# One transformer block on one core: instructions issued in a computed order instead of in the hand-written one

## The chip, the cores and the metric

The program runs on one core of one Trainium2 chip. The metric is the device time of one execution in microseconds (us), the median of several runs. The engines go by the names of the profile: PE (TensorE: matmuls and transposes), DVE (VectorE), ACT (ScalarE), POOL (GpSimd) and SP (SyncE, whose queue issues every DMA here). Each engine works through its own queue in order, and an instruction that waits for another engine or for a DMA holds up whatever stands behind it in the same queue.

## The reference

One block with a modulated layernorm, attention over the last 512 keys of a cache, and a gated feed-forward part. Shapes: x is 2048 x 512, 32 heads of 128, feed-forward width 1376.

```python
mod = (silu(c) @ w_mod).reshape(1, 6, 1, -1)
sa, ca, ga, sb, cb, gb = (mod[:, i] for i in range(6))
h = layernorm(x) * (1 + ca) + sa
q = (h @ wq).reshape(B, Sq, 32, 128).transpose(0, 2, 1, 3)
k, v = k_cache[:, :, -512:], v_cache[:, :, -512:]
p = softmax(q @ k^T * 128 ** -0.5)
x = x + ga * ((p @ v).transpose(0, 2, 1, 3).reshape(B, Sq, 4096) @ wo)
h = layernorm(x) * (1 + cb) + sb
x = x + gb * ((gelu(h @ w_gate) * (h @ w_up)) @ w_down)
```

## The kernel before

Every matrix operand is held as two 16-bit floats, a high part and the rest, and each product is made of three matmuls (high x high, high x low, low x high) of 128 x 128 weights with 512 columns. So lines come in threes: L422 to L424 (`q_proj`, the projection of q), L440 (`w_product`, the same by a Winograd scheme from the fourth group of heads on), L478 to L480 (`s_mm`, scores), L525 to L527 (`pv`, probabilities times v), L541 to L543 (`wo_mm`, output projection), L1008 to L1010 (gate and up) and L1035 to L1037 (`down`).

The 2048 rows are taken as four quarters of 512, the heads in groups of two: 128 iterations `it`, each one head and one quarter. For one half of an iteration (256 rows) `s_max` (DVE, L486, L488) finds the row maxima, `s_exp` (ACT, L497, L500) the exponentials and their high part, `s_low` (POOL, L505) the low part, and two DMA transposes (L510) turn the result, `pp`, into `pT`. `pv` uses `pT` two iterations later, `wo_mm` comes three iterations later, and `wo_add` (DVE, L551, L553) adds into the accumulators `acc`.

PSUM has two pairs of banks `psS` for scores, one bank `psQ`, one `psO` and two `psW`. Tiles with one tag share a ring of `bufs` buffers, in the order in which they are allocated.

The order of each engine's queue is the order of the program's text, and three things make that up by hand:

- `PLAN`, a list of steps with a time in half iterations. Steps at -1 are the lead-in: statistics of the first quarter (`stats`, L174 to L183), its normalisation (`norm`, L189, L194), its transposes (`turn0`, L601; later quarters `ln1_turn`, L199), the modulation as 64 one-column matmuls (`mod_mm`, L592), `cols_add`, `cols_bound` and `cols_scale` (L609 to L620), `chunk` (L571 to L576: the affine step and its split in two parts), and `warm` (L561): transposes of the identity into a bank of their own, whose result nobody reads, 54 of them at the front, then 2, 1 and 16 further back, the 16 straight ahead of the first `q_proj`. The other steps hang in the first eight iterations.
- `at(half, ...)` and `hooks`: loads of the next heads' weights, their maxima (`h_max`, L275), the crossings of partitions (`cross_a`, L152 to L154, and `cross_b`, L159 to L163), scaling (L355), splitting (L358, L359), the transposes of k (L328) and the feed-forward weights (L983 to L990), each at a fixed half iteration.
- `slot(i)`, which writes out one iteration's interleaving, and the loop behind it that does the feed-forward part.

The framework adds the semaphores between engines; it keeps each queue in the order given (`manual_schedule`).

Of the kernel before, what the change touches and what calls it, by code (L numbers as in the profile page):

```python
# [80 lines left out]
EARLY_CROSS = (7, 9)  # L81


@with_exitstack
def adaln_block(ctx: ExitStack, tc: tile.TileContext, x, k_cache, v_cache, wq, wo,
                w_gate, w_up, w_down, c_in, w_mod, out):
    nc = tc.nc
    x = x[0]
    out = out[0]
    koff = k_cache.shape[2] - W  # L90

    ctx.enter_context(tc.manual_schedule())
    ps = ctx.enter_context(tc.tile_pool(name="ps", bufs=1, space=PSUM))
    base = ctx.enter_context(tc.tile_pool(name="base", bufs=1, side="left"))

    def bank(tag, bufs=1):
        return ps.tile([P, N], F32, tag=tag, bufs=bufs, name=tag)
# [4 lines left out]
    def small(pool, cols_, bufs=3, name="sm"):  # L102
        return pool.tile([P, cols_], F32, name=name, tag=name, bufs=bufs)

    ident = base.tile([P, P], F32, name="ident")
    make_identity(nc, ident)
# [18 lines left out]
    mff = base.tile([P, 40], F32, name="mff")  # L125
    ffs = base.tile([P, 16], F32, name="ffs")

    left1 = tc.alloc_tile_pool(name="left1", bufs=1, side="left")

# [13 lines left out]
    right = tc.alloc_tile_pool(name="right", bufs=1, side="right")  # L143

    def raw_tile(tag="raw", bufs=8):
        return right.tile([P, N], F32, name=tag, tag=tag, bufs=bufs)
# [66 lines left out]


    csb = base.tile([P, NC], F32, name="csb")
    with nc.allow_non_contiguous_dma(reason="512 values"):
# [44 lines left out]
    e = small(base, NC, 1, "sil")  # L261
# [438 lines left out]
    for p in range(2):  # L700
        for c in range(2):
            n = 8 + 7 * (2 * p + c)
# [16 lines left out]
    for it in range(2, first_w):  # L719
        n = 2 * (it - 2)  # L720
# [45 lines left out]
    s = 36  # L766
    for j, r, f, a in ((4, ga, mod_to_cols, (colA[2], 1.0)), (3, gb, mod_to_cols, (colB[2], 0.0)),
# [4 lines left out]
        n = s + 9  # L772
# [64 lines left out]
    s = max(s, 2 * (NIT - 16))  # L837
# [58 lines left out]
    def x1_load(qg, j):  # L896
        t = 4 * qg + j
        if qg == 0:
            xr = raw_tile()
        else:  # L900
            if not XT:
                XT.append(right.tile([P, 4, N], F32, name="xr", tag="pT", bufs=3))
            xr = XT[0][:, j, :]
        XR[t] = xr
        nc.sync.dma_start(xr, x[t * P:(t + 1) * P, :])

    def x1_mul(qg, j, eng=nc.vector):
        t = 4 * qg + j
        eng.tensor_tensor(acc[t], acc[t], ga, op=OP.mult)

    def x1_add(qg, j, eng=nc.vector):
        t = 4 * qg + j
        eng.tensor_tensor(acc[t], acc[t], XR.pop(t), op=OP.add)

    def ln2_stats(qg, j):
        ln_stats(("2", qg), acc[4 * qg + j], j)

    def ln2_norm(qg, j):
        if j % 2 == 0:
            t = b_tile(1, ("T3", "T4")[j // 2], (P, 2, N), F32) if qg == 0 else \  # L920
                right.tile([P, 2, N], F32, name="n2", tag="pp", bufs=3)
            N2[qg, j], N2[qg, j + 1] = t[:, 0, :], t[:, 1, :]
        ln_norm(("2", qg), N2[qg, j], acc[4 * qg + j], j, nc.scalar if qg == 0 and j % 2 else None)


    def ln2_chunk(qg, c, eng=nc.scalar):
        if c == 0:
            if qg >= 2:
                H2[qg] = H2[qg - 2]
            elif qg == 0:  # L930
                H2[qg] = tuple(b_tile(0, nm, (P, NC, N)) for nm in ("B21", "T4"))
            else:
                t = right.tile([P, 2 * NC, N], F16, name="h2", tag="pT", bufs=3)
                H2[qg] = (t[:, :NC, :], t[:, NC:, :])
        key = ("2", qg)
        ln_pe(key, [N2[qg, j] for j in range(4)], c, pair()[:, 0, :] if qg else bank("psQ"))
        pt = LNP.pop((key, c))
        full = FULL[qg, c] = right.tile([P, N], F32, name="h32", tag="h32", bufs=3)
        a, b = colA[2][:, c:c + 1], colB[2][:, c:c + 1]
        if eng is nc.scalar:  # L940
            nc.scalar.activation(full, pt, AF.Identity, scale=a, bias=b)
# [152 lines left out]
    while nd < NU:  # L1094
        u = done[0] // (2 * NC)
        for _ in range(2):
            if nd < (u - 1 if u < NU else u):
                down(nd)
                nd += 1
        if u < NU:  # L1100
            qg, f = divmod(u, NF)
            if qg == 0:
                if f + 1 < NF:
                    ff_quick("g", f + 1)
                    ff_quick("u", f + 1)
                ff_quick("d", f)
                if f + 3 < NF:
                    ff_load(f + 3)
                if f + 2 < NF:
                    wd_load(f + 2)  # L1110
            fill(2 * NC)
            f0 = 3 if qg == 0 else 1
            if qg + 1 < NQG and f in (f0, f0 + 1):
                for j in (0, 1):
                    x1_load(qg + 1, 2 * (f - f0) + j)
            if qg + 1 < NQG and f in (f0 + 1, f0 + 2):
                for j in (0, 1):
                    x1_mul(qg + 1, 2 * (f - f0 - 1) + j)
                    x1_add(qg + 1, 2 * (f - f0 - 1) + j)
                    ln2_stats(qg + 1, 2 * (f - f0 - 1) + j)  # L1120
            if qg + 1 < NQG and f == 6:
                for j in range(4):
                    ln2_norm(qg + 1, j)
            if qg + 1 < NQG and f >= 7:
                c = f - 7
                ln2_chunk(qg + 1, c)
                ln2_high(qg + 1, c)
                ln2_low(qg + 1, c, nc.gpsimd if c % 2 else nc.vector)
    right.release()
    left1.release()  # L1130

# [27 lines left out]
```

## Time and profile before

| what | us |
|---|---|
| runs, median (lowest to highest of 3) | 1743.51 (1742.43 to 1746.09) |
| profiled execution, first to last instruction (span) | 1738.4 |
| what lies around the span: median less span | 5.1 |
| PE busy in the span | 1702.6 |
| DVE, ACT, POOL busy | 1197.4, 1099.5, 1061.7 |

No time of its own is given for the profiled execution, so its span is set beside the median of the runs. Busy time of PE is the union of its matmuls; a matmul of 512 columns takes about 380 ns from start to end, but the next one starts some 216 ns after it, so PE can be busy without a gap only when a matmul is always ready. "PEclk" is the share of the TensorE clock that was granted.

### The profile page before, as it was taken

To read this page: it belongs to the slowest core of one execution; us is meant where nothing else is said; L and a number is where in the kernel's file an instruction comes from. 1 tells how busy PE (TensorE), PEld (TensorE's weight loads), DVE (VectorE), ACT (ScalarE), POOL (GpSimd) and SP (SyncE) were. 2 spreads that over 40 slices of the span, in tenths; PEclk is the share of its full clock that TensorE was granted. 3 is DMA by queue.
4 is the path that set the end of the run, shared out by engine and by line. 5 is a ranking of instruction groups with operands and counts; after the bars stand their busy time and mean duration, and the time that the engine had idled before them with its cause. 6 is when DMAs were issued, how large, how long until landed. Compare 5 with 4: busy or idle time off the path is not lost.

```text
span 1738.4 us, 23741 instructions
## 1 busy us (share of the span) xinstructions
PE 1702.6 (98%) x7927; PEld 788.4 (45%) x7927; DVE 1197.4 (69%) x2292; ACT 1099.5 (63%) x2145; POOL 1061.7 (61%) x845
## 2 busy tenths in 40 slices
PE   8889999999999999999999999999999899999998
PEld 7434444444444444444444444444444344444443
DVE  5867767777778877787878787877877564424222
ACT  3866676777777778777777777777778534131311
POOL 2788896868776868686777767686869501101010
PEclk8999999999999999999999999999999999999999
DMA  6766767787878788787777777777677630101000
GB/s 200 138 119 114 148 122 150 151 163 140 149 139 155 140 151 146 139 161 142 160 142 154 138 156 146 151 142 144 127 153 140 121 97 26 49 1 49 1 25 25
DMA packets 658954, 213.55 MB, mean 123 GB/s; under 512 B 580304, under 2 KB 640720, under 8 KB 658832
## 3 DMA queue, kind: packets, MB, share of 16 engines
q1 hardware_dynamic: 658832, 212.03, 61.4%
q8 instruction: 63, 1.03, 0.2%
q14 instruction: 59, 0.48, 0.1%
HBM read 65.14 MB, written 4.19 MB: 40 GB/s over the span
## 4 chain that ended last, share of the span: by engine, by line
PE 67%; POOL 9%; ACT 9%; DVE 6%; issue 4%; DMA 3%; SPq 2%; ACTq 0%; DVEq 0%; POOLq 0%
PE psQ L440 9%; PE psS L1009 4%; PE psS L1008 4%; PE psS L1010 4%; PE psS L478 4%; PE psO L525 4%; PE psO L527 4%; PE psO L526 4%; PE psS L480 4%; PE psS L479 4%; POOL pp L505 4%; PE psW L541 4%; PE psW L542 4%; PE psW L543 4%; ACT p L497 3%
## 5 line engine op out<-in xcount | busy, mean ns | idle before, releaser
L505 POOL TENSOR_TENSOR pp<-p,pp 128x1024 f16<-128x1024 f32 x256 | 545.7, 2132 | 313.1 <-ACT pp L500 225.8
L497 ACT ACTIVATE p<-psS,st,es 128x512 f32<-128x512 f32 x512 | 393.0, 773 | 242.6 <-DVE st L488 239.5
L553 DVE SCALAR_TENSOR_TENSOR acc<-psW,st,acc 128x512 f32<-128x512 f32 x496 | 366.2, 742 | 27.4 <-PE psW L543 26.8
L486 DVE TENSOR_REDUCE st<-psS 128x2 f32<-128x1024 f32 x256 | 311.4, 1217 | 34.5 <-PE psS L480 34.1
L500 ACT ACTIVATE pp<-p 128x1024 f16<-128x1024 f32 x256 | 270.6, 1057 | 8.1
L525 PE MATMUL psO<-pT,v 128*128 128x512 f16 x512 | 194.3, 379 | 5.2 <-DVE mr L154 3.6
L478 PE MATMUL psS<-kT,q 128*128 128x512 f16 x512 | 194.9, 381 | 1.6 <-DMA kT<-k 1.6
L541 PE MATMUL psW<-wo,oT 128*128 128x512 f16 x512 | 194.5, 380 | 0.9 <-DVE acc L553 0.7
L480 PE MATMUL psS<-kT,q 128*128 128x512 f16 x512 | 194.5, 380 | 0.1
L479 PE MATMUL psS<-kT,q 128*128 128x512 f16 x512 | 194.5, 380 | 0.0
L542 PE MATMUL psW<-wo,oT 128*128 128x512 f16 x512 | 194.5, 380 | 0.0
L543 PE MATMUL psW<-wo,oT 128*128 128x512 f16 x512 | 194.3, 379 | 0.0
L526 PE MATMUL psO<-pT,v 128*128 128x512 f16 x512 | 194.3, 379 | 0.0
L527 PE MATMUL psO<-pT,v 128*128 128x512 f16 x512 | 194.2, 379 | 0.0
L1020 ACT ACTIVATE gl<-psS,ffs 128x512 f32<-128x512 f32 (+1 forms) x44 | 30.2, 687 | 211.6 <-PE psS L1010 211.6
L1021 DVE SCALAR_TENSOR_TENSOR gl<-psS,ffs,gl 128x512 f32<-128x512 f32 (+1 forms) x44 | 33.0, 750 | 176.8 <-ACT gl L1020 176.8
L531 ACT ACTIVATE oT<-psO 128x512 f16<-128x512 f32 x128 | 75.8, 592 | 68.2 <-PE psO L527 67.5
L534 DVE SCALAR_TENSOR_TENSOR oT<-psO,oT 128x512 f16<-128x512 f32 x128 | 88.2, 689 | 41.8 <-ACT oT L531 41.6
L275 DVE TENSOR_REDUCE mx<-raw 128x1 f32<-128x512 f32 x128 | 86.2, 676 | 42.6 <-DMA raw<-in_A_wq_dram 33.2
L440 PE MATMUL psQ<-T,S 128*128 128x512 f16 x468 | 113.7, 379 | 0.3 <-ACT h L452 0.3
L468 DVE SCALAR_TENSOR_TENSOR q<-psQ,q 128x512 f16<-128x512 f32 x50 | 34.5, 690 | 99.3 <-ACT q L465 99.2
L497 ACT ACTIVATION_READ_ACCUMULATOR p<-psS,st,es 128x1 f32 x512 | 100.5, 196 | 0.0
(258 smaller groups left out, 3009.9 us busy)
## 6 DMA issues: line engine op xcount, KB each, us to landing
raw<-in_A_wq_dram SPq DMA_DIRECT2D x32, 256.0 KB, 3.3
raw<-in_A_k_cache_dram SPq DMA_DIRECT2D x32, 256.0 KB, 3.4
raw<-in_A_v_cache_dram SPq DMA_DIRECT2D x32, 256.0 KB, 3.1
raw<-in_A_wo_dram SPq DMA_DIRECT2D x32, 256.0 KB, 2.9
pT<-pp SPq DMA_TRANSPOSE x512, 3.2
raw<-in_B_w_down_dram SPq DMA_DIRECT2D x20, 256.0 KB, 3.1
raw<-in_B_w_gate_dram SPq DMA_DIRECT2D x18, 256.0 KB, 3.6
raw<-in_B_w_up_dram SPq DMA_DIRECT2D x18, 256.0 KB, 3.7
```

The source lines that it names most:

```text
L440: nc.tensor.matmul(pq, x, y, start=first, stop=last, skip_group_check=True)
L478: nc.tensor.matmul(p[:, j, :], q[:, 0, qs], k[:, 0, :], start=True, stop=False)
L479: nc.tensor.matmul(p[:, j, :], q[:, 0, qs], k[:, 1, :], start=False, stop=False)
L480: nc.tensor.matmul(p[:, j, :], q[:, 1, qs], k[:, 0, :], start=False, stop=True)
L486: nc.vector.tensor_reduce(st[:, 2 * b:2 * b + 2], PSS[it, b], op=OP.max, axis=AX.X, negate=True)
L497: nc.scalar.activation(p32[:, j, :], p[:, j, :], AF.Exp, bias=st[:, n:n + 1], scale=ES[head_qg(it)[0]][:, 0:1], accum_out=st[:, 4 + n:5 + n])
L500: nc.scalar.activation(pp[:, :, 0, :], p32, AF.Copy)
L505: nc.gpsimd.tensor_tensor(pp[:, :, 1, :], p32, pp[:, :, 0, :], op=OP.subtract)
L525: nc.tensor.matmul(po, vh, pT[:, t, :], start=(t == 0), stop=False)
L541: nc.tensor.matmul(p, o[:, 0, ts], w[:, 0, :], start=True, stop=False)
L542: nc.tensor.matmul(p, o[:, 0, ts], w[:, 1, :], start=False, stop=False)
L553: nc.vector.scalar_tensor_tensor(a, p, r, a, op0=OP.mult, op1=OP.add)
```

## The change

The operations, their tiles and their sizes stay. All calls on engines go through an object `Weaver`, which notes them instead of issuing them, and tiles are allocated through it, so that it knows the rings. At the end `issue()` plays a schedule through on paper and then makes the real calls in the order found. Only the making of the identity is still issued at once. Cut to its core:

```diff
+class Weaver:
+    LAG, DRAIN, LANES = 60.0, 165.0, 8
+    NEXT = {"ACT": 95.0, "DVE": 85.0, "POOL": 45.0, "PE": 0.0, "SP": 0.0}
...
+    def cost(self, engine, what, a, k, n, names):
+        if engine == "PE":
+            wide = a[1].dtype == F32
+            return (110.0 if n > 8 else 60.0) * (...) if wide else max(n, 60) / 2.4 + 2.4
...
+        if engine == "ACT":
+            d = (150.0 if psum else 187.0) + 0.85 * n + (90.0 if "scale" in k and by else 0.0) + (85.0 if "bias" in k else 0.0)
+            return d + (95.0 if k.get("accum_out") is not None else 0.0)
+        if engine == "DVE":
+            return 165.0 + 30.0 * len(by) if small else (140.0 if what != "tensor_scalar" or psum else -60.0) + 1.06 * n + 50.0 * bool(by)
...
+        return (520.0 if k.get("op") == OP.pow else 180.0) + (1.92 if a[0].dtype == F16 else 2.13) * n
...
+    def note(self, engine, what, real, a, k):
...
+        d = 62.0 if engine == "SP" else self.cost(engine, what, a, k, n, [x.name for x in read])
+        self.ops.append((engine, d, deps, real, a, k, n))
+    def rank(self):
...
+        t, at = 0.0, []
+        for engine, d, *_ in self.ops:
+            at.append(t if engine == "PE" else 1e12)
+            t += d if engine == "PE" else 0.0
+        for n in reversed(line):
+            for m in self.ops[n][2]:
+                e, c = self.ops[m][:2]
+                lag = c if e == self.ops[n][0] == "PE" else c + self.LAG + (self.DRAIN if e == "PE" else 2600.0 if e == "SP" else 0.0)
+                at[m] = min(at[m], at[n] - lag)
+    def issue(self):
...
+        while len(order) < len(self.ops):
+            t, e = min((max(free[e], 0.0 if can[e] else wait[e][0][0]), e) for e in free if can[e] or wait[e])
...
+            n = heapq.heappop(can[e])[1]
+            order.append(n)
+            free[e] = t + d - self.NEXT[e]
+            end = t + d + self.LAG + (self.DRAIN if e == "PE" else 0.0)
+            if e == "SP":
+                if len(landed) >= self.LANES:
+                    t = max(t, landed[-self.LANES])
+                free[e] = t + d
+                bus = max(bus, t + 1350.0) + (size * 4 * 128 / 190.0 if whole else 1300.0)
+                end = max(bus, t + 2000.0) + 300.0
...
+        for n in order:
+            _, _, _, real, a, k, _ = self.ops[n]
+            real(*a, **k)
...
-    nc = tc.nc
+    nc = Weaver(tc.nc)
...
+    with nc.nc.allow_non_contiguous_dma(reason="512 values"):
+        nc.issue()
```

In words: `note` finds what an operation depends on from the ranges that it reads and writes (a PSUM tile counts as a whole), and `rank` adds that the first users of a tile wait for all users of the tile whose buffer it takes. An operation of PE is due at the sum of the costs of the matmuls ahead of it in the text; any other operation is due as late as lets its users keep their due times. In the schedule on paper an engine that comes free takes, of the operations whose inputs are there, the one due first. It never stays idle while it has one.

More of the change, by code (lines that the diff above doesn't have):

```diff
@@ L81, with __init__, __getattr__, tile @@
 EARLY_CROSS = (7, 9)
+class Weaver:
+    LAG, DRAIN, LANES = 60.0, 165.0, 8
+    NEXT = {"ACT": 95.0, "DVE": 85.0, "POOL": 45.0, "PE": 0.0, "SP": 0.0}
+    def __init__(self, nc):
+        self.nc = nc
+        for name, engine in (("vector", "DVE"), ("scalar", "ACT"), ("gpsimd", "POOL"), ("tensor", "PE"), ("sync", "SP")):
+            setattr(self, name, self.Port(self, engine, getattr(nc, name)))
+        self.ops, self.held, self.seen, self.before, self.rings, self.table = [], {}, {}, {}, {}, {}
+    class Port:
+        def __init__(self, weaver, engine, real):
+            self.weaver, self.engine, self.real = weaver, engine, real
+        def __getattr__(self, what):
+            return lambda *a, **k: self.weaver.note(self.engine, what, getattr(self.real, what), a, k)
+    class Pool:
+        def __init__(self, weaver, pool, whole):
+            self.weaver, self.pool, self.whole = weaver, pool, whole
+        def tile(self, shape, dtype, name=None, tag=None, bufs=1):
+            tag = tag or name
+            t = self.pool.tile(list(shape), dtype, name=name, tag=tag, bufs=bufs)
+            w, key = self.weaver, t.name
+            ring = w.rings.setdefault((id(self), tag), [])
+            w.before[key] = (ring[-bufs] if len(ring) >= bufs else None, ring[-1] if ring else None)
+            ring.append(key)
+            w.held[key], w.seen[key] = [], set()
+            if self.whole:
+                w.held[key].append(None)
+            return t
+        def release(self):
+            self.pool.release()
+    def pool(self, pool, whole=False):
+        return self.Pool(self, pool, whole)
+    @staticmethod
+    def extent(x):
+        n, hi = 1, 0
+        for s, c in list(x.ap)[1:]:
+            n, hi = n * c, hi + s * (c - 1)
+        step = list(x.ap)[0][0]
+        lo = x.offset % step if step else x.offset
+        return n, lo, lo + hi + 1
+    def cost(self, engine, what, a, k, n, names):
+        psum = any(m.startswith("ps") for m in names)
+        if engine == "PE":
+            wide = a[1].dtype == F32
+            return (110.0 if n > 8 else 60.0) * (1 if what == "transpose" or n <= 8 else n / 128) if wide else max(n, 60) / 2.4 + 2.4
+        small = n <= 16
+        by = [x for x in list(a[2:]) + list(k.values()) if hasattr(x, "ap") and self.extent(x)[0] == 1]
+        if engine == "ACT":
[3 more added lines that the diff above has]
+            return 165.0 + 30.0 * len(by) if small else (140.0 if what != "tensor_scalar" or psum else -60.0) + 1.06 * n + 50.0 * bool(by)
+        if what in ("tensor_scalar", "memset", "tensor_copy"):
+            return 170.0 + 1.03 * n
+        return (520.0 if k.get("op") == OP.pow else 180.0) + (1.92 if a[0].dtype == F16 else 2.13) * n
+    def note(self, engine, what, real, a, k):
+        op = len(self.ops)
+        wrote = [x for x in (a[0] if a else k["out"], k.get("accum_out")) if x is not None]
+        read = [x for x in list(a[1:]) + list(k.values()) if hasattr(x, "ap") and x is not k.get("accum_out")]
+        deps = set()
+        n = 1
+        for x, write in [(x, False) for x in read] + [(x, True) for x in wrote]:
+            m, lo, hi = self.extent(x)
+            n = max(n, m) if engine != "PE" else self.extent(wrote[0])[0]
+            key = x.name
+            held = self.held.get(key)
+            if held is None:
+                continue
+            if held[:1] == [None]:
+                lo, hi = -1, 1 << 30
+            for e in held:
+                if e and (write or e[3]) and e[0] < hi and lo < e[1]:
+                    deps.add(e[2])
+            if write:
+                held[:] = [e for e in held if not e or not (lo <= e[0] and e[1] <= hi)]
+            held.append((lo, hi, op, write))
+            self.seen[key].add(op)
+        if what == "activation" and a[2] not in (AF.Copy, AF.Identity):
+            for f, s in self.table.items():
+                if f != a[2]:
+                    deps |= s
+            self.table.setdefault(a[2], set()).add(op)
+        deps.discard(op)
+        d = 62.0 if engine == "SP" else self.cost(engine, what, a, k, n, [x.name for x in read])
+        self.ops.append((engine, d, deps, real, a, k, n))
+    def rank(self):
+        for key, (old, last) in self.before.items():
+            if self.seen[key]:
+                behind = (self.seen[old] if old else set()) | ({min(self.seen[last])} if last and self.seen[last] else set())
+                for n in [n for n in self.seen[key] if not self.ops[n][2] & self.seen[key]]:
+                    self.ops[n][2].update(behind)
+        users, left = [[] for _ in self.ops], [len(op[2]) for op in self.ops]
+        for n, op in enumerate(self.ops):
+            for m in op[2]:
+                users[m].append(n)
+        line = [n for n, k in enumerate(left) if not k]
+        for m in line:
+            for n in users[m]:
+                left[n] -= 1
+                if not left[n]:
+                    line.append(n)
+        assert len(line) == len(self.ops), "the tiles' rings close a circle"
+        t, at = 0.0, []
[7 more added lines that the diff above has]
+                at[m] = min(at[m], at[n] - lag)
+        return at, users
+    def issue(self):
+        import heapq
+        at, users = self.rank()
+        left, ready = [len(op[2]) for op in self.ops], [0.0] * len(self.ops)
+        wait = {e: [] for e in self.NEXT}
+        can = {e: [] for e in self.NEXT}
+        for n, op in enumerate(self.ops):
+            if not op[2]:
+                heapq.heappush(wait[op[0]], (0.0, n))
+        free, landed, bus, order = {e: 0.0 for e in self.NEXT}, [], 0.0, []
+        while len(order) < len(self.ops):
+            t, e = min((max(free[e], 0.0 if can[e] else wait[e][0][0]), e) for e in free if can[e] or wait[e])
+            while wait[e] and wait[e][0][0] <= t:
+                n = heapq.heappop(wait[e])[1]
+                heapq.heappush(can[e], (at[n], n))
+            n = heapq.heappop(can[e])[1]
+            order.append(n)
+            _, d, _, _, a, k, size = self.ops[n]
+            free[e] = t + d - self.NEXT[e]
[4 more added lines that the diff above has]
+                free[e] = t + d
+                whole = self.ops[n][3].__name__ == "dma_start"
+                bus = max(bus, t + 1350.0) + (size * 4 * 128 / 190.0 if whole else 1300.0)
+                end = max(bus, t + 2000.0) + 300.0
+                landed.append(end)
+            for m in users[n]:
+                ready[m] = max(ready[m], t + d if e == "PE" == self.ops[m][0] else end)
+                left[m] -= 1
+                if not left[m]:
+                    heapq.heappush(wait[self.ops[m][0]], (ready[m], m))
+        for n in order:
+            _, _, _, real, a, k, _ = self.ops[n]
+            real(*a, **k)
@@ L92, in adaln_block @@
     ctx.enter_context(tc.manual_schedule())
-    ps = ctx.enter_context(tc.tile_pool(name="ps", bufs=1, space=PSUM))
-    base = ctx.enter_context(tc.tile_pool(name="base", bufs=1, side="left"))
+    ps = nc.pool(ctx.enter_context(tc.tile_pool(name="ps", bufs=1, space=PSUM)), True)
+    base = nc.pool(ctx.enter_context(tc.tile_pool(name="base", bufs=1, side="left")))
     def bank(tag, bufs=1):
@@ L105, in adaln_block @@
     ident = base.tile([P, P], F32, name="ident")
-    make_identity(nc, ident)
+    make_identity(nc.nc, ident)
     identb = base.tile([P, 8], BF16, name="identb")
@@ L126, in adaln_block @@
     ffs = base.tile([P, 16], F32, name="ffs")
-    left1 = tc.alloc_tile_pool(name="left1", bufs=1, side="left")
+    left1 = nc.pool(tc.alloc_tile_pool(name="left1", bufs=1, side="left"))
     BN = ("B11", "T2", "T1", "B22", "T3", "T4", "B21")
@@ L141, in h_view @@
         return t[:, 0, c % 2, :], t[:, 1, c % 2, :]
-    right = tc.alloc_tile_pool(name="right", bufs=1, side="right")
+    right = nc.pool(tc.alloc_tile_pool(name="right", bufs=1, side="right"))
     def raw_tile(tag="raw", bufs=8):
@@ L215, in adaln_block @@
     csb = base.tile([P, NC], F32, name="csb")
-    with nc.allow_non_contiguous_dma(reason="512 values"):
+    if True:
         nc.sync.dma_start(csb, c_in.rearrange("o (k p) -> p (o k)", p=P))
```

## The prediction

> **What bounds the kernel now.** I read the engines' shares first, then a table of stages, then what PE waits for in each.
>
> ```profile
> PE 1702.6 (98%) x7927; PEld 788.4 (45%) x7927; DVE 1197.4 (69%) x2292; ACT 1099.5 (63%) x2145; POOL 1061.7 (61%) x845
> core 0: us, PE busy (x) PEld busy (x) DVE busy (x) ACT busy (x) POOL busy (x), PEclk, DMA share, GB/s
> 0.00:30.10 30.10, 27.84 (x157) 26.77 (x158) 14.12 (x39) 6.66 (x10) 5.37 (x19) 0.72 0.95 288
> 30.10:125.00 94.90, 82.51 (x379) 37.75 (x380) 75.25 (x156) 70.01 (x132) 70.37 (x64) 0.96 0.60 114
> 125.00:1350.00 1225.00, 1216.13 (x5635) 548.29 (x5634) 955.46 (x1858) 913.82 (x1832) 933.87 (x718) 1.00 0.76 145
> 1350.00:1395.00 45.00, 39.12 (x176) 17.59 (x174) 25.91 (x46) 21.70 (x39) 23.24 (x20) 0.96 0.56 112
> 1395.00:1732.00 337.00, 336.99 (x1585) 158.03 (x1583) 123.50 (x193) 87.27 (x135) 27.35 (x25) 1.00 0.10 32
> 1732.00:1738.40 6.40, 0.00 (x0) 0.00 (x0) 3.19 (x4) 0.00 (x0) 1.44 (x2) 0.83 0.44 164
> ```
>
> After each stage's length stand the busy times of PE, its weight loads, DVE, ACT and POOL, then the granted clock. PE is the bound: from 125 to 1350 us it runs 1216.13 of 1225 us, 215.8 ns for each of 5635 instructions, and in the feed-forward part, 1395 to 1732 us, it has no gap at all. The work is the same after the change, so an order can win only what PE loses. It loses, in idle time, 12.4 us in the first iterations (30.1 to 125), 8.9 in the long middle and 5.9 around 1350 to 1395, where attention hands over to the feed-forward part. The clock of 0.96 costs about 0.04 x 94.9 = 3.8 and 0.04 x 45 = 1.8 us more in two of these stages. That is 32.8 us in all, 1.9% of the span: the ceiling outside the lead-in. The lead-in, 30.1 us until the first q projection, and the last 6.4 us are chains of dependencies.
>
> What PE waits for in the three stages, in the same order (us in total, times, longest); the longest lines:
>
> ```profile
> PE psQ L422 <- DVE q L468: 3.5, 2, 3.3
> PE psQ L423 <- POOL B L576: 2.4, 2, 1.2
> PE psO L159 <- DVE oT L534: 1.1, 1, 1.1
> ...
> PE psO L525 <- DVE mr L154: 3.6, 7, 1.1
> PE psQ L422 <- DVE q L468: 3.3, 4, 1.3
> ...
> PE psQ L199 <- ACT h L941: 2.9, 2, 2.7
> PE psO L525 <- DMA pT<-pp: 1.4, 1, 1.4
> ```
>
> These are waits of position: a crossing put into PE's queue a little ahead of the reduction it needs (`mr` L154, seven times in the middle, 3.6 us), a q projection before the bank is free, a transpose of the second layernorm into a bank that ACT has still to read. Behind each stand matmuls of other banks.
>
> **The change, part by part.** Operations removed or added: none, so that term is zero. *PE's own order.* A PE operation is due at its place in the old text, so PE keeps that order unless the next one isn't ready on paper, and then takes the next that is. That is what the positional waits call for. Data waits (L423 on POOL's halves of the affine step, 2.4 us) stay unless POOL does these sooner.
>
> *The costs on paper* decide how good the order is, since the queues stay strict. Against the rows:
>
> ```profile
> L505 POOL TENSOR_TENSOR pp<-p,pp 128x1024 f16<-128x1024 f32 x256 | 545.7, 2132 | 313.1 <-ACT pp L500 225.8
> L553 DVE SCALAR_TENSOR_TENSOR acc<-psW,st,acc 128x512 f32<-128x512 f32 x496 | 366.2, 742 | 27.4 <-PE psW L543 26.8
> L486 DVE TENSOR_REDUCE st<-psS 128x2 f32<-128x1024 f32 x256 | 311.4, 1217 | 34.5 <-PE psS L480 34.1
> L500 ACT ACTIVATE pp<-p 128x1024 f16<-128x1024 f32 x256 | 270.6, 1057 | 8.1
> 32.99 1.02 POOL L179 TENSOR_TENSOR rs<-ve,eps_t 128x4 f32<-128x4 f32 x1
> L510 SPq DMA_TRANSPOSE pT<-pp x10: 1232/1328/1587, 700.0 to 723.2; - x10
> ```
>
> The formulas give 180 + 1.92 x 1024 = 2146 ns against 2132, 140 + 1.06 x 512 + 50 = 733 against 742, 140 + 1.06 x 1024 = 1225 against 1217 and 187 + 0.85 x 1024 = 1057 against 1057: within 2% for the work that fills the middle. Two are off. The power of L179 is 520 + 2.13 x 4 = 529 ns on paper and 1.02 us in the trace, a few times, early. And SP is given 62 ns an issue, where a transpose holds its queue 1.3 us; the schedule has the 1.3 us in its bus (1300 ns each), so landings come out nearly right, but SP may commit to an order too early.
>
> *The middle, 125 to 1350 us.* The margin that a wrong order would eat is that between a landed `pT` and its first use, here one of 128:
>
> ```profile
> 719.72 2.13 POOL L505 TENSOR_TENSOR pp<-p,pp 128x1024 f16<-128x1024 f32 x1 [3.33 <-issue]
> 721.87 2.62 SPq L510 DMA_TRANSPOSE pT<-pp  x2
> DMA to landing us min/median/max: 3.2/3.3/5.0
> 730.21 0.38 PE L525 MATMUL psO<-pT,v 128*128 128x512 f16 x1
> ```
>
> Issued by 721.87 + 2.62 = 724.49, landed by about 727.8, used at 730.21: 2.4 us. POOL, DVE and ACT are busy 76%, 78% and 75% of this stage, so a queue that is wrong by one operation (1 to 2 us) still fits. I take 6 us of the 8.9 as removed and 3 us as new waits where an operation was placed just when paper had it ready: -3. Bounds: -8.9 (all gone) to +26 (0.25 us more in each of 128 iterations, which is 32, less the 6).
>
> *The lead-in.* Here the change has a definite cost. The 19 later `warm` transposes depend only on the identity, so on paper they are ready from the start, and PE, which may not idle, runs all 73 at once while the first loads are under way. The rows:
>
> ```profile
> 1.35 8.20 PE L561 MATMUL psQ<-ident 128*128 128x128 f32 x54 [1.35 <-POOL ident masks.py:199]
> 9.69 2.81 PE L592 MATMUL psS<-silu,wm 128*128 128x1 f32 x24
> 13.01 1.87 PE L592 MATMUL psS<-silu,wm 128*128 128x1 f32 x8 [0.37 <-DVE mr L154]
> 23.76 0.17 DVE L609 TENSOR_TENSOR cols<-psS,plus 128x8 f32<-128x8 f32 x1 [5.97 <-PE psS L592]
> 26.59 3.37 PE L561 MATMUL psQ<-ident 128*128 128x128 f32 x16
> 30.32 0.38 PE L423 MATMUL psQ<-T,A 128*128 128x512 f16 x1
> 67.11 0.58 PE L423 MATMUL psQ<-B,A 128*128 128x512 f16 x1 [1.16 <-POOL B L576]
> 25.00:30.00 5.00, 4.95 (x25) 4.71 (x23) 4.39 (x13) 3.73 (x6) 2.81 (x3) 0.54 0.93 148
> 30.00:35.00 5.00, 4.37 (x20) 1.70 (x20) 3.81 (x9) 1.98 (x5) 1.95 (x7) 1.00 0.00 0
> ```
>
> At 152 ns each (8.20 / 54), 73 end at 12.4 instead of 9.55 us. The first modulation matmul then starts up to 2.7 us later; but these run at 117 ns (2.81 / 24) while the clock is up and at 234 ns (1.87 / 8) once it has fallen, some 3.5 us after the transposes end, so the later end buys that back and `cols` (23.76) comes about when it did. What is not bought back: the 16 transposes at 26.59 no longer precede the first q projection. The last two rows, 5 us windows in the columns of the table of stages, show the clock go from 0.54 to 1.00 by 30 us behind them. Without them q's 12 matmuls and the first scores start at half speed (0.58 against 0.38 us for one, starts 0.43 apart). For 3.4 to 6.8 us at half speed I count 1.7 to 3.4 us lost, and take +2.5; bounds 0 (the first projection comes sooner by another order) to +6 (loads or `norm` misplaced by paper's slower loads too). The Trainium skill, page "TensorE: Matmul & The Clock Gate", Part 1, says the half clock is the default, lifted after one busy window of about 3.4 us and restored after an idle one; the 3.37 us of transposes ahead of 30.1 agree, and by that rule alone the loss would be at the 1.7 us end.
>
> *The first iterations, 30.1 to 125 us.* ACT, DVE and POOL are three quarters busy here, so part of PE's 12.4 us is plain lack of data. Ordering by due time puts layernorm work of later quarters behind that of the next; of 12.4 + 3.8 I take 4.5, bounds 0 to 11.
>
> *The hand-over.* Waits on L941 and `pT`, 2.9 + 1.4 us, are positional and gate matmuls are there to fill: of 5.9 + 1.8 I take 3.5, bounds 0 to 7. *The feed-forward part and the end*: PE has no gap and DVE and ACT are under 40%; zero.
>
> Sum: -3 + 2.5 - 4.5 - 3.5 = -8.5, a span of 1729.9 and, with the 5.1 us between span and median, **1735 us**.
>
> **Rivals.** *Slower by new waits in the middle.* If real landings or POOL's halves come later than on paper by more than the 2.4 us margin, `pv` waits in its strict queue and with it all of PE, in each iteration alike. It decides from 11.5 / 128 = 0.09 us an iteration, since the other three terms give 5.5 and the middle's 6 are gained as well. At 0.15 to 0.25 us it adds 19 to 32 us to -11.5: 1751 to 1764. For it: SP's 62 ns against 1.3 us, and a margin of 2.4 us that two such misplaced issues use up. Against: costs within 2%, and three engines idle a quarter of the stage.
>
> *Slower by the start.* Paper has loads, the modulation matmuls (60 ns against 117 to 234) and the power wrong just where every step is on the path. With +6 for the lead-in, the first iterations 5 us longer and only 2 won later, it is about 1752.
>
> *Nearly no change.* Since PE is due in the old order, it may keep it and the old waits with it; gains of 3 to 4 pay the half-speed start: 1740 to 1747.
>
> *Nearly all of it.* The greedy order closes most gaps and the clock dips with them: -8 in the middle, -9 early, -6 at the hand-over, +2.5: -20.5, 1723.
>
> **How the numbers follow.** A change of 0.2%, 3.5 us, is about what a measurement of this kernel can tell from none. The forecast (1727 to 1740) has 0.40, nearly all of it 0.13, nearly no change 0.12, new waits in the middle 0.22, a slower start 0.13. So faster 0.53, same 0.12, slower 0.35. The forecast's own range is 1727 to 1740; the range over all cases is 1723 to 1758, from the full gain to the mid of the new waits, which leaves out about 0.06 below and 0.11 above.
>
> **What would show it.** Right: all `warm` in one run at the front; a clock of 0.5 in the first q projection; the waits on `mr` L154 gone; idle PE time under 5 us from 125 to 1350 and under 4 around the hand-over; the feed-forward part still 337 us. Wrong: a first q projection after 34 us, PE waiting on `pT` or on `kT` in every iteration, or an idle time of PE in the middle above 12 us.

## The result, and the profile after

The computed order is slower: 1749.13 us median (1747.10 to 1752.56, 9 runs) against 1744.10 (1742.43 to 1747.12, 9 runs), ratio 1.0031 [1.0021, 1.0042]. The span shown is 1746.3 us in an execution of 1748.06, so 1.8 us lie around a span, and the profile shown before (1738.4) was an execution some 4 us quicker than its median if as much lies around it. Spans differ by 7.9 us, medians by 5.0.

The engines' shares and the stages after, in the columns of before:

```profile
PE 1698.6 (97%) x7927; PEld 785.7 (45%) x7927; DVE 1213.4 (69%) x2292; ACT 1081.5 (62%) x2145; POOL 1069.3 (61%) x845
...
0.00:30.10 30.10, 24.59 (x157) 24.08 (x158) 11.84 (x35) 3.68 (x6) 3.12 (x19) 0.76 0.85 271
30.10:125.00 94.90, 76.64 (x348) 35.48 (x348) 77.03 (x146) 69.34 (x131) 80.03 (x68) 0.92 0.51 104
125.00:1350.00 1225.00, 1216.91 (x5645) 548.40 (x5644) 963.51 (x1864) 899.06 (x1831) 927.07 (x714) 1.00 0.76 146
1350.00:1395.00 45.00, 36.24 (x164) 16.38 (x163) 44.50 (x73) 28.45 (x53) 28.13 (x20) 0.96 0.75 168
1395.00:1740.00 345.00, 344.22 (x1619) 161.40 (x1616) 114.53 (x178) 80.98 (x127) 30.08 (x26) 1.00 0.08 23
```

PE starts 348 operations in the first iterations where it started 379: 31 x 0.216 = 6.7 us lost, by more idle time (18.3 us in place of 12.4) and a lower clock (0.92 in place of 0.96). It wins 10 in the middle (2.2 us) and loses 12 at the hand-over (2.6 us); 7.1 of the 7.9. DVE is full at the hand-over, 44.50 of 45 us in place of 25.91.

What PE waits for, in the first iterations, the middle and the hand-over (every operation now has the line of the helper that issues it, so one goes by tiles):

```profile
PE psS L245 <- DVE mx L245: 4.6, 1, 4.6
PE psQ L245 <- ACT T L245: 3.9, 1, 3.9
PE psW L245 <- DVE h L245: 3.8, 2, 2.6
...
PE psO L245 <- DMA pT<-pp: 7.7, 12, 1.4
...
PE psW L245 <- DVE oT L245: 4.0, 1, 4.0
PE psW L245 <- DVE acc L245: 3.5, 4, 1.3
```

The waits on `mr` and `q` are gone from the middle; `pT` has taken their place. The 4.6 us on `mx`, the maxima of the second head's k, hold up the first scores because these maxima cross partitions in the PSUM bank that the scores take next. The wait goes back to SP's queue. On SP, DVE and PE in the timeline after (start, length):

```profile
23.52 0.43 SPq L245 DMA_DIRECT2D raw<-in_A_k_cache_dram  x1
44.13 0.66 DVE L245 BATCH_NORM_STATS2 bnst<-acc 128x6 f32<-128x512 f32 x1
44.93 0.65 DVE L245 TENSOR_REDUCE mx<-raw 128x1 f32<-128x512 f32 x1
45.64 0.38 PE L245 MATMUL psS<-ident,mx 128*8 128x128 f32 x1 [4.57 <-DVE mx L245]
46.51 2.74 PE L245 MATMUL psS<-kT,q 128*128 128x512 f16 x6
```

The same load and the maxima before:

```profile
12.97 0.38 SPq L239 DMA_DIRECT2D raw<-in_A_k_cache_dram  x1
27.91 1.27 DVE L275 TENSOR_REDUCE mx<-raw 128x1 f32<-128x512 f32 x2
```

The second head's k is loaded 10.6 us later, its maximum stands in DVE's queue behind statistics of later quarters, and the first scores start at 46.51 in place of 33.54. The load itself landed 4.0 us after its issue, at 27.5, so the data lay there for 17 us. The schedule on paper, played through again, shows why: at 190 bytes per ns, and with the load ahead of it in the ring taken for a landing to wait for, it has this load land only at 38.8 us of its own clock, and gives DVE other work until then.

At the hand-over the 4.0 us on `oT` come from what stands ahead of it in DVE's queue: two splits of feed-forward weights (4.17 us, 1.5 on paper) and three products for a later quarter (1.88 us). ACT had delivered its half of `oT` at 1372.47.

```profile
1371.36 4.17 DVE L245 SCALAR_TENSOR_TENSOR T<-raw,ffs,T 128x512 f16<-128x512 f32 x2
1371.89 0.58 ACT L245 ACTIVATE oT<-psO 128x512 f16<-128x512 f32 x1
1375.46 1.88 DVE L245 TENSOR_TENSOR acc<-acc,ga 128x512 f32<-128x512 f32 x3
1377.26 0.68 DVE L245 SCALAR_TENSOR_TENSOR oT<-psO,oT 128x512 f16<-128x512 f32 x1
1378.00 1.04 PE L245 MATMUL psW<-wo,oT 128*128 128x512 f16 x2 [4.00 <-DVE oT L245]
```

### The profile page after: what moved, and what is told of

The parts are those of the page before. It is cut to its first block, busy times and chain, and to the rows that moved or that the text cites. A ratio compares the mean times of both kernels' runs of the same rounds, so it can differ in the third digit from the quotient of the medians.

```text
span 1746.3 us, 23696 instructions
## 1 busy us (share of the span) xinstructions
PE 1698.6 (97%) x7927; PEld 785.7 (45%) x7927; DVE 1213.4 (69%) x2292; ACT 1081.5 (62%) x2145; POOL 1069.3 (61%) x845
## 4 chain that ended last, share of the span: by engine, by line
PE 84%; DVE 6%; POOL 3%; DMA 3%; ACT 2%; issue 1%; SPq 0%; DVEq 0%; POOLq 0%; ACTq 0%
PE psS L245 30%; PE psW L245 19%; PE psO L245 19%; PE psQ L245 16%; DMA pT<-pp 3%; DVE st L245 2%; DVE acc L245 2%; POOL pp L245 1%; ACT p L245 1%; SPq L245 0%; ACT pp L245 0%; DVE mx L245 0%; DVE B L245 0%; POOL tf L245 0%; POOL A L245 0%
## 5 line engine op out<-in xcount | busy, mean ns | idle before, releaser
L245 PE MATMUL psW<-wo,oT 128*128 128x512 f16 x1536 | 416.4, 379 | 8.8 <-DVE oT L245 4.0
L245 PE MATMUL psS<-kT,q 128*128 128x512 f16 x1536 | 389.6, 381 | 1.1 <-DMA kT<-k 1.1
L245 PE MATMUL psO<-pT,v 128*128 128x512 f16 x1536 | 370.4, 379 | 8.1 <-DMA pT<-pp 7.7
L245 PEld LDWEIGHTS <-oT 128*128 128x128 f16 x1536 | 149.9, 98 | 190.9 <-issue 7.1
L245 PEld LDWEIGHTS <-v 128*128 128x128 f16 x1536 | 149.0, 98 | 192.8 <-issue 10.3
L245 PEld LDWEIGHTS <-q 128*128 128x128 f16 x1536 | 148.3, 98 | 173.3 <-issue 3.2
L245 PE MATMUL psQ<-B,A 128*128 128x512 f16 x528 | 130.2, 380 | 1.5 <-DVE q L245 1.5
L245 PEld LDWEIGHTS <-A 128*128 128x128 f16 x756 | 74.4, 99 | 97.1 <-issue 8.1
L245 PEld LDWEIGHTS <-B 128*128 128x128 f16 (+1 forms) x744 | 72.9, 98 | 86.0 <-issue 0.3
L245 POOL TENSOR_TENSOR q<-h,q 128x512 f16<-128x512 f32 x78 | 90.2, 1157 | 13.8 <-ACT q L245 13.2
```

What stands on the lines that cost most here:

```text
L245: real(*a, **k)
```

## The experiments

All are the changed kernel with the edit named. "PE" is its operations from 30.1 to 125 us and from 1350 to 1395, "pT" its waits on `pT` in the middle (us, times). These two columns come from one execution each and move with the clock that it was granted: e8 and e11 have the same order until the last iterations, and their 377 and 359 operations differ with a clock of 0.95 and 0.91. So in the first iterations a difference of some 18 operations tells nothing by itself. By time, two runs are told apart where their intervals don't overlap.

| run | edit | median (range), us | ratio to before | PE | pT |
|---|---|---|---|---|---|
| before | | 1744.10 | 1 | 379, 176 | |
| change | | 1749.13 (1747.10 to 1752.56) | 1.0031 [1.0021, 1.0042] | 348, 164 | 7.7, 12 |
| e1 | ring order of first loads soft | 1747.02 (1746.31 to 1749.21) | 1.0017 [1.0008, 1.0025] | 346, 161 | 7.8, 11 |
| e2 | hand lead-in, with e1 | 1739.87 (1737.59 to 1743.35) | 0.9972 [0.9961, 0.9984] | 377, 162 | 7.5, 11 |
| e3 | hand end | 1747.93 (1743.88 to 1749.41) | 1.0018 [1.0009, 1.0028] | 344, 175 | 7.8, 12 |
| e4 | `warm` in place | 1747.24 (1744.08 to 1748.97) | 1.0014 [1.0005, 1.0022] | 351, 161 | 7.0, 10 |
| e5 | Winograd work held | 1747.24 (1745.44 to 1751.01) | 1.0019 [1.0010, 1.0028] | 347, 167 | 5.7, 7 |
| e6 | e1 + e4 + e5 | 1743.08 (1742.03 to 1744.90) | 0.9991 [0.9983, 1.0000] | 363, 166 | 4.5, 6 |
| e7 | e2 + e3 | 1738.83 (1736.03 to 1741.08) | 0.9966 [0.9952, 0.9979] | 386, 182 | 7.6, 10 |
| e8 | load rate 385 | 1738.25 (1735.06 to 1741.03) | 0.9964 [0.9951, 0.9978] | 377, 179 | 2.6, 5 |
| e9 | load rate 260 | 1739.99 (1735.10 to 1741.55) | 0.9968 [0.9956, 0.9981] | 382, 179 | 3.0, 9 |
| e10 | load rate 2000 | 1746.76 (1743.38 to 1750.92) | 1.0012 [1.0002, 1.0023] | 374, 163 | 3.0, 8 |
| e11 | e8 + e3 | 1736.49 (1732.23 to 1740.06) | 0.9950 [0.9934, 0.9966] | 359, 181 | 3.3, 9 |
| e12 | e8 + e3 + e6 | 1730.10 (1728.26 to 1731.60) | 0.9917 [0.9904, 0.9931] | 390, 187 | 2.9, 7 |
| e13 | e11 + e4 | 1736.93 (1734.37 to 1738.11) | 0.9962 [0.9950, 0.9974] | 369, 182 | 3.0, 6 |
| e14 | e11 + e5 | 1732.31 (1731.09 to 1736.73) | 0.9942 [0.9929, 0.9954] | 388, 184 | 3.4, 8 |
| e15 | e12, `pT` lands 0.6 us sooner on paper | 1725.45 (1724.81 to 1729.76) | 0.9897 [0.9882, 0.9911] | 382, 192 | 0.7, 2 |
| e16 | e12, 0.8 us later | 1735.92 (1732.48 to 1740.55) | 0.9959 [0.9943, 0.9975] | 398, 178 | 3.3, 5 |
| e17 | change, 0.6 us sooner | 1740.56 (1737.86 to 1742.66) | 0.9977 [0.9967, 0.9988] | 355, 160 | none listed |
| e18 | e12, 1.2 us sooner | 1729.13 (1725.92 to 1730.03) | 0.9906 [0.9893, 0.9920] | 387, 194 | 2.0, 2 |

The times of e2, e8, e11, e12, e15 and e17 came out 0.5 to 3.8 us below every range that was expected of them, and that of e18 lies in the range of a draw, above that of theory N. The runs below show directions; their sizes were mostly misjudged.

**Where it is lost, e1 to e4.** The first theory: paper takes the order in a ring of load buffers for a landing to wait for, and so holds back the loads. The edits: a ring edge counts as met when the load ahead is issued (e1); each operation up to the end of the first eight iterations (e2, which carries e1's edit too) or of the end (e3) stays behind the one ahead of it in the text on its engine; the 19 later `warm` are tied to the PE operation ahead of them (e4).

```diff
+   if last and key.startswith("raw_") and n < 39:   # e1
+       m = min(self.seen[last])
+       if not old or m not in self.seen[old]:
+           self.soft.add((m, n))
...
+   if i == 8:                                       # e2
+       nc.keep.append((0, len(nc.ops)))
...
+   if i == NIT + 0:                                 # e3
+       nc.keep.append((len(nc.ops), 1 << 30))
...
+   nc.ops[-1][2].update(ahead)                      # e4
```

> The changed kernel lost about 7 us by 125 us of the span. Theory A (a ring's order is taken for a wait: on paper each of the first eight raw loads starts only when the raw load ahead of it in the ring has landed, so k of head 1 is issued behind the x tiles of later quarters and its maximum stands behind their statistics on DVE): with that wait on paper made an order only for the first eight raw loads, k of head 1 goes out before the x tiles of quarters 2 and 3, the first score matmul starts at 36 to 39 us instead of 46.5, the 4.6 us wait of PE on the maximum is gone, and the time falls by 3 to 7 us, to 1742 to 1746. Theory B (the half clock and the transposes without result at the front are what costs): the first score matmul may come sooner, but the time stays within 2 us of 1749. Theory C (DVE and POOL are simply overloaded in the first 125 us by a greedy order): PE's wait moves to the next operand, time within 2 us of 1749.

> The first eight iterations and all ahead of them keep the hand-written order on each engine; the rest is computed. If the loss is all in the start and in the hand-over, the first 125 us come out as before (first q projection at 30.1, first scores at 33.5, some 12 us of PE idle from 30 to 125) and the time is 6 to 8 us below the changed kernel, 1741 to 1743, of which the hand-over still holds about 3 us of loss. If the middle had lost as well, it would stay above 1746.

> From the slot after the last scores on (slot 128), each engine keeps the hand-written order; all before is computed. Theory D (at the hand-over the computed order lets DVE take splits of feed-forward weights and products for later quarters as soon as they are ready, 44.5 of 45 us busy, and PE waits 4.0 us for oT and 3.5 us for acc behind them): the idle PE time from 1350 to 1395 falls from 8.8 to 6 us or less and the time falls by 2 to 4 us, to 1745 to 1747. If the waits only move to the splits that now come later, the time stays within 1 us of 1749.

> The 19 later transposes without result are tied to the PE operation that stands ahead of them in the text, so 16 of them again run just ahead of the first q projection. The prediction gave this 2.5 us (1.7 to 3.4 lost at half speed). If it is on the path: q's 12 matmuls at 0.22 us apart instead of 0.43 and the time falls by 2 to 3 us. Rival: the first scores wait for the maximum of k of head 1 in any case, at 45 us, so the faster q only lengthens that wait and the time stays within 1 us of 1749.

The place is the lead-in with the first iterations: e2 wins 9.3 us and is faster than before. The ring is not its cause alone: in e1 the first scores start at 40.55 and the 4.6 us on `mx` are gone, but the time falls by 2.1 us only. (That PE starts no more operations than in the change tells little: this execution was slower than most of e1, with a clock of 0.88 there in place of 0.92, and PE's idle time did fall, from 18.3 to 15.8 us.) e1, e3 and e4 are worth 1 to 2 us each, near the limit of what can be told.

**Early work or wrong prices, e5 to e8.** In the change POOL does 12 Winograd sums and splits between 30 and 90 us, which a matmul first uses at 281 us in the kernel before; e5 lets each start only once the PE operation ahead of it in the text has. e8 changes one number:

```diff
-   bus = max(bus, t + 1350.0) + (size * 4 * 128 / 190.0 if whole else 1300.0)
+   bus = max(bus, t + 1350.0) + (size * 4 * 128 / 385.0 if whole else 1300.0)
```

> The Winograd sums and splits of the weights (t_full, t_sum, t_split) may start only when the PE operation that stands ahead of them in the text has started on paper; all else is the computed order. Theory D (early work in the way): in the trace after, POOL does 12 of these operations, 15.7 us, between 30 and 90 us, in place of lower halves, and DVE's two-input operations are longer beside them; without them POOL's 80.0 us in the stage 30.1 to 125 fall to about 70, DVE's 77.0 to about 74, PE has 355 to 365 matmuls there in place of 348, and the time is 1743 to 1746. Theory W (one wait sets the lead-in): the first scores still wait for the maxima of k until about 46 us, PE has at most 350 matmuls in the stage and the time is 1748 to 1749.

> Three restraints together: the ring order of the first raw loads no longer counts as a landing to wait for, the 19 later warm transposes keep their place behind the PE operation ahead of them in the text, and the Winograd sums and splits are held as in the run beside it. Theory D: the three causes add, the first scores start before 37 us, PE has 370 matmuls or more from 30.1 to 125, and the time is 1740 to 1743. Theory O (too much ready at once): with the first wait gone another takes its place, since DVE, ACT and POOL are ordered by due times that rest on wrong costs; 350 to 360 matmuls, 1744 to 1747.

> The hand order on every engine for the lead-in with the first eight iterations, and again from the end of the attention loop on; the computed order between them. If the two losses are separate (the hand lead-in alone was 9.3 us under the computed order, the hand end alone 1.2 us), the time is 1738 to 1739, PE has about 377 matmuls from 30.1 to 125 and 175 from 1350 to 1395, and the feed-forward splits no longer fill DVE there (26 us in place of 43). If the end only passes its loss on, 1740 as with the hand lead-in alone.

> One number is changed: a load's rate on paper, 190 to 385 bytes per ns (the trace before moves 385 to 392 GB/s in the slices where its DMA is full); the rules stay. Theory P (wrong prices): with the loads at the rate of the chip, paper commits queues in an order that fits real landings, and the ring rule costs half as much; the first scores come before 40 us in place of 46.5, PE has 360 or more matmuls from 30.1 to 125, the time is 1742 to 1745. Theory G (the rule, work is taken as soon as it is ready): the order changes but early work still stands ahead of urgent work in the strict queues; 1747 to 1751.

e6 adds up: 6.0 us against 2.1, 1.9 and 1.9. What the hand end is worth in time stays open: it takes 1.2 us off the change (e3) and 1.0 us off e2 (e7), less than the intervals can tell. e8 alone does as much as both hand orders: at the right price of a load the computed order is faster than the hand-written one, so this price accounts for more than the whole loss. Paper now has the second head's k landed at 20.0 us, and DVE takes its maximum at 31.71 in place of 44.93. Its first iterations, its middle and its hand-over, the first scores now at 35.18:

```profile
30.10:125.00 94.90, 81.64 (x377) 37.84 (x376) 79.44 (x153) 68.76 (x133) 78.87 (x66) 0.95 0.55 111
125.00:1350.00 1225.00, 1219.69 (x5654) 549.46 (x5653) 968.30 (x1869) 905.76 (x1843) 934.32 (x717) 1.00 0.77 147
1350.00:1395.00 45.00, 39.85 (x179) 17.98 (x179) 43.94 (x74) 24.93 (x43) 19.25 (x18) 0.96 0.66 153
```

At the hand-over DVE is as full as in the change (43.94 us), yet PE waits 0.5 us for `oT` in place of 4.0. So a full DVE alone doesn't cost it; what stands ahead of the urgent operation does.

The rate of the chip is in the kernel before, 5 to 25 us, last column:

```profile
5.00:25.00 20.00, 19.23 (x119) 18.38 (x118) 8.26 (x22) 1.33 (x2) 1.23 (x2) 0.69 1.08 364
```

**A trend or a lucky draw, e9 to e12.** The same line with 260 and 2000; e8 with the hand end, and with the three restraints of e6.

> The load rate on paper is 260 bytes per ns, between the 190 of the change and the 385 of the trace; nothing else. Theory P (the wrong price is the cause): the result lies between the two, 1741 to 1746, with the first scores between 37 and 44 us; since the paper margin between a landed pT and its use is 0.5 us in the median here (0.2 at 190, 0.6 at 385), the waits of PE on pT in the middle are 2 to 5 us. Theory L (any other order is a draw, and 385 was a lucky one): no relation to the rate, anything from 1738 to 1750.

> The load rate on paper is 2000 bytes per ns, far above the chip's. Theory P: the price is wrong again, the other way, paper believes in weights and maxima that have not landed: the first scores come later than the 35.2 us of the run at 385, fewer than 377 matmuls from 30.1 to 125, 1740 to 1745. Theory U (only underrating the loads does harm, since a load that is thought early costs only the wait it would cost anyway): 1737 to 1740. Theory L: no relation.

> Rate 385 on paper, and the hand order on every engine from the end of the attention loop on. If the hand-over's loss is separate, as it was at 190 (1.2 us) and with the hand lead-in (1.0 us), the time is 1737 to 1738 and PE has 180 matmuls or more from 1350 to 1395, with DVE near 26 us there. Rival: at this rate the computed hand-over has no loss left (179 matmuls against 176 in the kernel before), and the hand order gives 1738 to 1740.

> Rate 385, the three restraints of the earlier run (ring order of the first raw loads not taken as a landing, warm transposes in their old place, Winograd sums and splits held) and the hand order at the end. Theory P: with the right price the restraints have little left to mend, 1737 to 1739. Theory D (early work still in the way): the restraints take another 3 to 5 us, 1733 to 1736, with the first scores before 35 us and 385 matmuls or more from 30.1 to 125.

190, 260, 385, 2000 give 1749.1, 1740.0, 1738.3, 1746.8: good around the chip's rate, where 260 and 385 can't be told apart, and worse on either side, which speaks against a draw. At 2000 the first iterations hardly suffer (374 operations, though the first scores wait until 41.00); most of the loss against e8 is in the middle (10.5 us idle in place of 5.3) and at the hand-over (163 operations in place of 179). And the restraints still win 6.4 us with the right price.

**Which restraint, e13 and e14.** One of them each, on e11.

> Rate 385 and the hand end as before, and of the three restraints only the 19 later warm transposes, tied to the PE operation ahead of them in the text. If the warm transposes are the lead-in's cost (the prediction's 2.5 us; alone at rate 190 they gave 1.9), the first q projection no longer starts at half the clock and the time is 1733 to 1735. If the Winograd work is, 1736 to 1737.

> Rate 385 and the hand end, and of the three restraints only the Winograd sums and splits held back. If they are in the way of urgent work on POOL and DVE in the first iterations, 1731 to 1733, with 370 matmuls or more from 30.1 to 125 where the run without had 359. If the warm transposes are the cause, 1736 to 1737. At rate 190 this restraint alone gave 1.9 us.

By the medians, holding the Winograd work gives 4.2 us and the place of `warm` nothing. The intervals of e11, e13 and e14 overlap, so that this work is the main part of the 6.4 us is likely and not shown, and the rest was not taken apart.

**The waits on `pT`, e15 to e18.** One number, the landing of the transposes:

```diff
-   end = max(bus, t + 2000.0) + 300.0
+   end = max(bus, t + 2000.0) + 300.0 + (0.0 if whole else -600.0)   # e16: 800.0, e18: -1200.0
```

> The best kernel so far (1730.1) with one number changed: paper takes the DMA transposes to land 0.6 us sooner. Theory M (the margin on paper between a landed pT and its first use, less what paper is wrong by, sets the waits): a twentieth of the iterations has a margin of 0.2 us on paper, which is 0.4 us too little by the trial before, so PE waits on pT more often and longer than the 7 times and 2.9 us there: 6 to 15 us in the middle, and the time is 1733 to 1742. Theory X (those few waits come from something else, as queues late by chance): 2 to 4 us, 1729 to 1732.

> The same with the transposes landing 0.8 us later on paper. Theory M: every pT is at least 0.8 us early against the trial before, so PE's waits on pT in the middle fall to 1 us or less; paper itself puts 7 us more idle time into PE, from places it could not fill (26.0 against 19.4 us), of which the chip may show a part: 1729 to 1735. Theory X: 2 to 4 us of waits on pT stay.

> The changed kernel with only the landing of the transposes on paper 0.6 us sooner (load rate 190 as in the change). Theory N (a pT that paper takes as landed early is placed by its due time and not at the moment it is ready, so that other work stands between; the median margin on paper goes from 0.2 to 0.8 us): PE's waits on pT in the middle fall from 7.7 to 2 us or less and the time is 1743 to 1746, the lead-in being as bad as before. Theory X (the waits on pT are late queues by chance): 5 to 8 us remain, 1747 to 1750.

> The best kernel so far (1725.5) with the landing of the transposes 1.2 us sooner on paper in place of 0.6. Theory N: the due times decide already, the order hardly changes (paper margins 0.25, 0.84 and 2.9 us at the 5th, 50th and 95th per cent, 0.22, 0.84 and 2.8 before), 1724 to 1728 and waits on pT of 2 us or less in the middle. Theory M, in its first form (each 0.1 us of margin less costs waits): 10 us of waits or more, 1735 or above. Theory L (a draw): 1728 to 1735.

The theory of the margin, that `pv` waits where paper leaves too little time behind a landing, fell: sooner on paper gave fewer waits, later did not take them away. Nor is the landing nearest to the chip the best: paper's shortest is 2.95 us after the issue (1350 + 1300 + 300 ns), the trace of the change has 3.3 in the median, and e17's 2.35 is further off and yet better by 8.6 us. The middle of e17, and the only wait listed there:

```profile
125.00:1350.00 1225.00, 1224.18 (x5688) 553.94 (x5688) 974.89 (x1887) 908.22 (x1849) 936.29 (x719) 1.00 0.78 147
```

```profile
PE psW L245 <- DVE acc L245: 0.7, 3, 0.3
```

0.82 us idle in 1225. Why the waits go is not settled. In the computed orders, of the 128 first `pv` matmuls of an iteration 53 stand later among PE's operations in the change than in the text, 23 in e17, 2 in e15, none in e18, and 126 in e16. One reading: a `pT` not landed on paper when its `pv` is due makes PE take other work, and `pv` then comes at the very moment that paper has it ready; landed early, it keeps the text's distance. But e12 has 23 as well, with 2.9 us of waits where e17 has none, and e16 with 126 waits less than the change with 53. So the count doesn't set the waits. Nor can e15 be told from e12 or e18 by time.

## Why the prediction was wrong

- *Costs on paper* is the step that failed. It set compute prices and the transposes' 1300 ns against rows, and those held to 2% in the rows shown, but not the loads' 190 bytes per ns, though the table of stages that it quoted shows 288 GB/s in the lead-in. It names slower loads on paper only within the lead-in's bound of +6 and gives them nothing in the other terms. That number cost 10.9 us (e8), and not at the start alone: in e8 the first scores come 11.3 us sooner, PE's waits on `pT` in the middle fall from 7.7 to 2.6 us, and its wait on `oT` at the hand-over from 4.0 to 0.5.
- *First iterations*, -4.5, bounds 0 to -11: measured +6.7, outside them. Ordering by due time was to put work of later quarters behind that of the next. It does so only among operations that paper has ready, and paper had k's maximum ready at 38.8 us where its data landed at 27.5, so statistics of later quarters went ahead. The rival "slower by the start" had the mechanism and, within 3 us, the time, though not the place: it gave the lead-in +6.
- *Lead-in*, +2.5: the first projection came 1.2 us later (31.26) and at half clock, as said (0.59 us a matmul). Two details were wrong: the 73 `warm` ran as 41, 23 and 9 with modulation matmuls between them, and `cols` came at 26.31, not when it did (23.76). e4's 1.9 us at rate 190 fits the size without showing it; at 385 nothing is seen (e13).
- *Middle*, -3: PE's idle time went from 8.9 to 8.1. All of the old waits went, not 6 us, and 7.7 came on `pT`, not 3. The rival "new waits" was right in kind; it counted 128 iterations and there were 12 waits. e17 shows that nearly the whole 8.9 was to be had.
- *Hand-over*, -3.5: measured +2.6. Gate matmuls were to fill the gaps, but PE waited for `oT` behind feed-forward splits and products that were ready and due later.
- *Feed-forward part*, zero: right. *Span to median*, 5.1: 1.8 of it lies around the span, the rest was a quick execution.
- None of the three signs of being wrong that it named came (31.26 us for the first projection, 12 waits on `pT`, 8.1 us idle in the middle): they watched the lead-in and the middle, and the loss was in the first iterations and at the hand-over.

## What to carry to other kernels

An order computed from prices is as good as its worst price: set each constant, the DMA rate above all, against the trace before the order is judged, since one number was worth 11 us here. Then sweep it on the chip: for the landing of the transposes, a value further from the trace was the better one (e17). A rule that takes whatever is ready also needs a reason to hold back work that is due much later. With the price, the three restraints, the hand end and early landings, the same operations run in 1725 to 1729 us (e15, e18).

## What the runs showed of the hardware

The clock in the lead-in can differ between executions of one order. e8 and e11 have the same order there; in the second the granted clock fell during these 24 matmuls and stayed at half for 20.5 us in place of 13.7. e8, then e11:

```profile
15.78 2.84 PE L245 MATMUL psS<-silu,wm 128*128 128x1 f32 x24 [0.26 <-DVE iv L245]
27.62 0.59 PE L245 MATMUL psQ<-T,A 128*128 128x512 f16 x1 [4.29 <-ACT T L245]
```

```profile
16.28 4.83 PE L254 MATMUL psS<-silu,wm 128*128 128x1 f32 x24 [0.26 <-DVE iv L254]
30.75 0.59 PE L254 MATMUL psQ<-T,A 128*128 128x512 f16 x1 [4.29 <-ACT T L254]
```

A start 0.5 us later became 3.1. The Trainium skill, page "TensorE: Matmul & The Clock Gate", Part 1, says that the windows run freely and the number of slow matmuls differs from run to run; this agrees.

A DVE operation with two inputs in SBUF stretches beside POOL. In the change, a split of v, 0.72 us before:

```profile
69.50 2.68 DVE L245 SCALAR_TENSOR_TENSOR v<-raw,av,v 128x512 f16<-128x512 f32 x1
69.51 2.12 POOL L245 TENSOR_TENSOR pp<-p,pp 128x1024 f16<-128x1024 f32 x1
```

It ends 0.55 us after POOL's. The Trainium skill, page "SBUF — State Buffer", "SBUF: two separate sides", calls this a lock on a shared port for a whole instruction; the trace agrees, and paper has no such price.
